# Attention with its q and k projections in plain fp32 instead of three fp32r products

## The chip, the cores and the metric

The kernel runs on one core of one Trainium2 chip. The metric is the device time of one execution in microseconds; the median of three runs of the kernel before is 1016.85 us. A profile is of one execution, with its own span and its own time.

## The reference

Only the first of three stages is touched. q, k and v are 4 x 8 x 576 x 64 (batch, heads, positions, head size), w_phi is 64 x 128:

```python
def phi(x):
    proj = np.einsum('bhsd,df->bhsf', x, w_phi)
    proj = proj - np.max(np.abs(proj), axis=-1, keepdims=True)
    return np.concatenate([np.exp(proj), np.exp(-proj)], axis=-1)
q_p, k_p = (phi(q), phi(k))
kv = np.einsum('bhsf,bhsd->bhfd', k_p, v)
z = np.sum(k_p, axis=2)
num = np.einsum('bhsf,bhfd->bhsd', q_p, kv)
den = np.einsum('bhsf,bhf->bhs', q_p, z)[..., None] + 1e-06
```

num / den, laid out as 2304 tokens of 512, goes through two feed-forward stages: relu(x w_in) squared times w_out (hidden size 2048), then sigmoid(x w_gate) * (x w_val) times w_out2 (hidden size 1536).

## The kernel before

Attention goes over 16 pairs of heads (4 batches, 4 pairs each; one pass of the loop over `n` is called an iteration here). Of a pair's 576 positions of k, 512 are taken as 4 x 128; the last 64 of all 8 heads of a batch are gathered in `kr` and done once a batch, in the first of its four iterations.

An iteration issues, in this order: `q_exp` of pair n (subtract the maximum, two exponentials); `proj_ks` and `proj_qs` of pair n + 1; `trans` of pair n + 2 (transposes of q and k on TensorE); `kv` of pair n (L373 and L380); `num` of pair n - 1 (L403 and L410, then the division on VectorE and GpSimd); `kv_tr` (L390); the loads of pair n + 3; in some iterations a weight conversion for the next stage (`convert1`) or a split of the attention output (`xsplit`), both mostly on VectorE. That is the order of the program; the framework then orders the instructions of each engine by a simulated timeline, so the code for the engines is fixed before the run.

A transposed tile stands in PSUM and is taken out by `split_evac`: ScalarE copies it rounded to fp32r (L289), VectorE subtracts that from the tile in PSUM and writes the rest, also fp32r (L290). So `qT`, `kT` and `krT` have two parts, and so have the weights `wq` and `wk`. A projection multiplies in three `passes`: high by high, high by low, low by high.

* `proj_k` (L347, three to six instructions each): one tile of 128 positions for two heads is the stationary operand (all 128 rows, 128 columns), and the weights move, 256 columns, set in blocks so that each half of the rows meets its own head's columns. Two such products of three passes make one `proj_k`: 6 instructions. There are 32 of them and 4 more for the remainder.
* `proj_q` (L326): for each of the two halves `e` of the positions the weights are stationary (64 rows, 128 columns) and 288 columns move. The two halves lie in partitions 0 to 63 and 64 to 127. 6 instructions for a head, 32 heads.

Everything else of attention is already plain fp32: L373, L380, L403, L410, the transposes L298, L305, L313 and L390, and the warm-up L258. All attention products use one pool of 8 PSUM banks (`bank`), so a product may have to wait until a bank is free. `proj_q` is taken out of PSUM by ScalarE (L329), `proj_k` by VectorE (L352, L353).

The feed-forward stages (L530, L551, L603, L707) follow, in fp32r with three passes, and are not touched.

Of the kernel before, what the change touches and what calls it, by code (L numbers as in the profile page):

```python
# [9 lines left out]
F32 = mybir.dt.float32  # L10
F32R = mybir.dt.float32r
U32 = mybir.dt.uint32
AF = mybir.ActivationFunctionType
ALU = mybir.AluOpType
# [5 lines left out]
def attention_moe_moe2(ctx, tc, q, k, v, w_phi, w_in, w_out, w_gate, w_val, w_out2, out):  # L20
    nc = tc.nc
    B, H, S, D = q.shape
    F = w_phi.shape[1]
    NT, DM = out.shape
    P = 128
# [20 lines left out]
    passes = ((0, 0), (0, 1), (1, 0))  # L46
    TINY = (2.0 ** -15 * 1.125) ** 2

    def f(ap):
        return ap.bitcast(F32)  # L50
# [8 lines left out]
    def bank(n):  # L59
        return ps.tile([P, 512], F32, tag="a", name="a")[:, :n]  # L60
# [30 lines left out]
    def split(hi, lo, src, hi_eng=nc.vector):  # L91
        if hi_eng is nc.scalar:
            nc.scalar.activation(hi, src, AF.Copy)  # L93
        else:
            hi_eng.tensor_copy(hi, src)
        last_g[0] = nc.vector.tensor_tensor(lo, src, f(hi), ALU.subtract)  # L96
# [120 lines left out]
    with ExitStack() as actx:  # L217
        cst = actx.enter_context(tc.tile_pool(name="cst", bufs=1))
# [3 lines left out]
        tp = tctx.enter_context(tc.tile_pool(name="tp", bufs=2, side="right"))  # L222
# [12 lines left out]
        for i in range(4):  # L235
            sl = slice(32 * i, 32 * i + 32)
            nc.vector.tensor_copy(ident[sl, sl], ramp[sl, 2])
        wst = cst.tile([P, F], F32, name="wst")
        for e in range(2):
            nc.scalar.dma_start(out=wst[e * D:(e + 1) * D, :], in_=w_phi)  # L240
        wq = cst.tile([P, 2, F], F32R, name="wq")
        split(wq[:, 0], wq[:, 1], wst)
        ones = cst.tile([P, 32], F32, name="ones")
        nc.vector.memset(ones, 1.0)
        zr = cst.tile([P, F], F32, name="zr")
        nc.vector.memset(zr, 0.0)
        wk = cst.tile([P, 2, 2, F], F32R, name="wk")
        for x in range(2):
            for e in range(2):
                nc.vector.tensor_copy(wk[:, x, e, :], zr)  # L250
        for x in range(2):
            for e in range(2):
                sl = slice(e * D, (e + 1) * D)
                nc.vector.tensor_copy(wk[sl, x, e, :], f(wq[sl, x, :]))

        warm = bank(P)
        for _ in range(NWARM):
# [26 lines left out]

        tT = {}

        def split_evac(pst, nm, key, bufs):
            t = tp.tile([P, 2, pst.shape[1]], F32R, tag=nm, name=nm, bufs=bufs)
            nc.scalar.activation(t[:, 0], pst, AF.Copy)  # L289
            nc.vector.tensor_tensor(t[:, 1], pst, f(t[:, 0]), ALU.subtract)  # L290
            tT[key] = t

        def trans_k(b, j):
            pt = bank(512)
            a = nat["k", b, j]
            for c in range(4):
                e, r = divmod(c, 2)
                nc.tensor.transpose(pt[:, c * P:(c + 1) * P], a[:, e, 2 * r:2 * r + 2, :], ident)  # L298
            split_evac(pt, "kT", ("k", b, j), 2)

        def trans_q(b, h):
            pt = bank(SH)
            a = nat["q", b, h // 2]
            for r in range(3):
                nc.tensor.transpose(pt[:, r * P96:(r + 1) * P96], a[:, h % 2, 2 * r:2 * r + 2, :], ident[:P96, :P96])  # L305
            split_evac(pt, "qT", ("q", b, h), 4)

        def trans_rem(b):
            a = nat["kr", b]
            pt = bank(NJ * SR)  # L310
            for j in range(NJ):
                o = (j % 2 * 2 + j // 2) * SR
                nc.tensor.transpose(pt[:, o:o + SR], a[:, 2 * j:2 * j + 2, :], ident[:SR, :SR])  # L313
            split_evac(pt, "krT", ("kr", b), 1)

        qx = {}
        mx = {}
# [2 lines left out]
        def proj_q(b, h):  # L320
            t = tT["q", b, h]
            pps = [bank(SH) for e in range(2)]
            for n, (x, y) in enumerate(passes):
                for e in range(2):
                    sl = slice(e * D, (e + 1) * D)
                    nc.tensor.matmul(pps[e], lhsT=wq[sl, x, :], rhs=t[sl, y, :], start=n == 0, stop=n == 2)  # L326
            for e in range(2):
                a = qpp.tile([P, 2, SH], F32, tag="qe", name="qe", bufs=12)
                nc.scalar.activation(a[:, 1, :], pps[e], AF.Copy)  # L329
                m = qpp.tile([P, SH], F32, tag="m", name="m", bufs=4)  # L330
                nc.gpsimd.partition_all_reduce(m, a[:, 1, :], channels=P, reduce_op=bass_isa.ReduceOp.absmax)  # L331
                qx[b, h, e] = a
                mx[b, h, e] = m
# [9 lines left out]
        def proj_k(t, o, key, tag, bufs):  # L343
            pp = bank(512)
            for r in range(2):
                for n, (x, y) in enumerate(passes):
                    nc.tensor.matmul(pp[:, r * 256:(r + 1) * 256], lhsT=t[:, x, o + r * P:o + (r + 1) * P],  # L347
                                     rhs=wk[:, y].rearrange("p a f -> p (a f)"), start=n == 0, stop=n == 2)
            a = pp.rearrange("p (c f) -> p c f", c=4)
            t = php.tile([P, 4, 2, F], F32, tag=tag, name=tag, bufs=bufs)  # L350
            m = sm.tile([P, 4, 1], F32, tag="km", name="km", bufs=3)
            nc.vector.tensor_reduce(m, a, AX.X, ALU.max, apply_absolute_value=True)  # L352
            nc.vector.tensor_tensor(t[:, :, 1, :], a, m.to_broadcast([P, 4, F]), ALU.subtract)  # L353
            nc.scalar.activation(t[:, :, 0, :], t[:, :, 1, :], AF.Exp)
            nc.scalar.activation(t[:, :, 1, :], t[:, :, 1, :], AF.Exp, scale=-1.0)
            ph[key] = t
# [76 lines left out]
        def trans(n):  # L433
            b, j = divmod(n, NJ)
            for e in range(2):
                trans_q(b, 2 * j + e)
            trans_k(b, j)
            if j == 0:
                trans_rem(b)

        def proj_qs(n):
            b, j = divmod(n, NJ)
            for e in range(2):
                proj_q(b, 2 * j + e)

        def proj_ks(n):
            b, j = divmod(n, NJ)
            for e in range(2):
                proj_k(tT["k", b, j], e * 256, (b, 2 * j + e), "ph", 4)
            if j == 0:  # L450
                proj_k(tT["kr", b], 0, ("r", b), "phr", 2)
# [16 lines left out]
        for n in range(B * NJ):  # L468
            b, j = divmod(n, NJ)
# [384 lines left out]
```

## Time and profile before

| | |
|---|---|
| median of 3 runs | 1016.85 us (1013.15 to 1017.01) |
| profiled execution, its own time | 1013.1 us |
| its span in the trace | 1011.3 us |
| TensorE (PE) busy | 991.6 us, 98% |
| VectorE (DVE) busy | 747.3 us, 74% |
| ScalarE (ACT) busy | 601.7 us, 59% |
| GpSimd (POOL) busy | 109.7 us, 11% |
| attention, until the first L530 | 198.5 us of the span |

The 1.8 us between the span and the time of the same execution lie outside the trace. A plain fp32 product appears in the trace as two PE MATMUL records (and two weight loads), an fp32r product and a transpose as one. Records of PE overlap, since matmuls are pipelined: the pace of PE is read from start to start, not from the duration of one.

### The profile page before, as it was taken

How to read it: one execution, taken by the hardware profiler on the slowest of the kernel's cores; microseconds unless marked ns; L12 is line 12 of the kernel's file. 1: busy time of each engine (PE TensorE's matmuls, PEld its weight loads, DVE VectorE, ACT ScalarE, POOL GpSimd, SP SyncE). 2: the span in 40 equal slices, each digit the busy share in tenths (PEclk: the TensorE clock that was granted, in tenths of full speed). 3: DMA queues.
4: the chain of work that ended last, by engine and by line, in shares of the span. 5: the costliest groups of instructions: out<-in, count | busy, mean ns of one | idle time of the engine just before them, and what ended most of it. 6: DMA issues, size and time to landing. Idle time of an engine off the chain costs nothing.

```text
span 1011.3 us, 17524 instructions
## 1 busy us (share of the span) xinstructions
PE 991.6 (98%) x6488; PEld 870.3 (86%) x6488; DVE 747.3 (74%) x1296; ACT 601.7 (59%) x1081; POOL 109.7 (11%) x196
## 2 busy tenths in 40 slices
PE   7999999999999999999999999999999999999996
PEld 6666666599999999889998899998899988999985
DVE  6799998869885987986969769856565656566532
ACT  6888878556555786446864466654465644555431
POOL 4556655400000000000000000000000000000000
PEclk9999999999999999999999999999999999999999
DMA  9444521349984576565775556632444422544302
GB/s 236 127 134 141 160 76 57 113 156 351 304 293 141 183 254 191 167 200 186 260 226 171 177 167 205 189 118 74 118 142 133 124 77 64 166 125 135 96 11 62
DMA packets 116406, 159.56 MB, mean 158 GB/s; under 512 B 12768, under 2 KB 74848, under 8 KB 116320
## 3 DMA queue, kind: packets, MB, share of 16 engines
q1 hardware_dynamic: 115680, 157.58, 49.8%
q8 instruction: 51, 0.84, 0.3%
q10 hardware_dynamic: 640, 0.85, 0.2%
q14 instruction: 35, 0.29, 0.1%
HBM read 125.37 MB, written 33.03 MB: 157 GB/s over the span
## 4 chain that ended last, share of the span: by engine, by line
PE 94%; DVE 3%; ACT 2%; POOL 0%; issue 0%; ACTq 0%
PE d L603 38%; PE d L551 20%; PE d L707 15%; PE d L530 7%; PE a L373 3%; PE a L410 3%; PE a L347 2%; PE a L380 2%; PE a L403 2%; PE a L326 1%; PE a L305 1%; PE a L390 1%; PE a L298 1%; ACT qe L329 0%; PE a L258 0%; ACT c L609 0%
## 5 line engine op out<-in xcount | busy, mean ns | idle before, releaser
L603 PE MATMUL d<-xs,hl 128*128 128x384 f32 x2184 | 385.4, 337 | 3.6 <-ACT c L609 3.6
L603 PEld LDWEIGHTS d<-xs,hl 128*128 128x128 f32 x2184 | 379.4, 188 | 6.6 <-ACT c L609 4.9
L138 DVE TENSOR_TENSOR hl<-wf,hl 128x512 fp32r<-128x512 f32 x282 | 192.4, 687 | 75.5 <-ACT hl L137 74.5
L137 ACT ACTIVATE hl<-wf 128x512 fp32r<-128x512 f32 x282 | 175.0, 626 | 88.5 <-PE d L603 48.3
L551 PE MATMUL d<-ghi,hl 128*128 128x256 f32 (+1 forms) x768 | 190.7, 338 | 0.0
L551 PEld LDWEIGHTS d<-ghi,hl 128*128 128x128 f32 x768 | 131.8, 188 | 16.3
L551 PE MATMUL d<-glo,hl 128*128 128x512 f32 (+1 forms) x384 | 128.5, 338 | 0.0
L707 PE MATMUL d<-hl,ghi 128*128 128x512 f32 x432 | 126.7, 395 | 0.0
L93 ACT ACTIVATE ghi<-G 128x768 fp32r<-128x768 f32 x48 | 40.7, 847 | 99.3 <-PE d L707 56.0
L707 PEld LDWEIGHTS d<-hl,ghi 128*128 128x128 f32 x432 | 80.9, 188 | 18.2
L96 DVE TENSOR_TENSOR glo<-G,ghi 128x768 fp32r<-128x768 f32 x48 | 46.0, 958 | 57.4 <-ACT ghi L93 56.9
L609 ACT ACTIVATE c<-d 128x768 f32<-128x768 f32 x78 | 61.3, 809 | 44.8 <-PE d L603 44.6
L331 POOL PARTITION_ALL_REDUCE m<-qe x64 | 83.5, 1375 | 35.5 <-ACT qe L329 33.3
L632 DVE TENSOR_TENSOR c<-c,d 128x768 f32<-128x768 f32 x54 | 51.2, 953 | 41.1 <-ACT c L609 26.8
L551 PEld LDWEIGHTS d<-glo,hl 128*128 128x128 f32 x384 | 72.3, 188 | 8.6
L707 PE MATMUL d<-hl,glo 128*128 128x512 f32 x216 | 76.3, 395 | 0.0
L530 PE MATMUL d<-xs,hl 128*128 128x384 f32 x384 | 69.1, 337 | 0.0
L530 PEld LDWEIGHTS d<-xs,hl 128*128 128x128 f32 x384 | 66.7, 188 | 1.1 <-issue 0.4
L115 ACT ACTIVATE st<-st 128x512 f32<-128x512 f32 x68 | 45.5, 678 | 32.4 <-DVE w L112 29.8
L707 PEld LDWEIGHTS d<-hl,glo 128*128 128x128 f32 x216 | 40.6, 188 | 9.8
L112 DVE SCALAR_TENSOR_TENSOR w<-st,w 128x512 uint32<-128x512 uint32 x68 | 46.6, 698 | 0.2
L113 DVE SCALAR_TENSOR_TENSOR w<-st,w 128x512 uint32<-128x512 uint32 x68 | 46.4, 693 | 0.5
(109 smaller groups left out, 1134.4 us busy)
## 6 DMA issues: line engine op xcount, KB each, us to landing
wf<-wd SPq DMA_DIRECT2D x84, 256.0 KB, 3.0
wf<-smd SPq DMA_DIRECT2D x72, 256.0 KB, 3.1
st<-in_moe_w_out_dram SPq DMA_DIRECT2D x28, 512.0 KB, 5.2
wf<-gvd SPq DMA_DIRECT2D x54, 256.0 KB, 3.2
wf<-wid SPq DMA_DIRECT2D x46, 256.0 KB, 4.3
st<-in_moe_w_in_dram SPq DMA_DIRECT2D x16, 512.0 KB, 5.9
wf<-ismd SPq DMA_DIRECT2D x32, 256.0 KB, 3.2
wd<-w SPq DMA_DIRECT2D x28, 256.0 KB, 3.4
```

Of the source, the lines that this page charges most:

```text
L96: last_g[0] = nc.vector.tensor_tensor(lo, src, f(hi), ALU.subtract)
L112: nc.vector.scalar_tensor_tensor(b, hi, 0xC0000000, b, ALU.bitwise_and, ALU.bitwise_or)
L113: nc.vector.scalar_tensor_tensor(b, lo, 29, b, ALU.logical_shift_right, ALU.bitwise_or)
L137: nc.scalar.activation(d[:, 0], a, AF.Copy)
L138: nc.vector.tensor_tensor(d[:, 1], a, f(d[:, 0]), ALU.subtract)
L331: nc.gpsimd.partition_all_reduce(m, a[:, 1, :], channels=P, reduce_op=bass_isa.ReduceOp.absmax)
L530: nc.tensor.matmul(pp[:, i, :n], lhsT=w[:, x, j, :], rhs=xs[j][:, y, o:o + n], start=k == 0, stop=k == 3 * NJ - 1)
L551: nc.tensor.matmul(acc[j][i], lhsT=w[:, x, j, :], rhs=a[y][:, o:o + n], start=c == 0 and k == 0 and (i == 0 or j % 2 == 0), stop=c == C1 - ...
L603: nc.tensor.matmul(acc[k, q][:, m], lhsT=w[:, i, 2 * m + kt, :], rhs=v[:, j, kt, :], start=start and n == 0, stop=n == 5, skip_group_check ...
L609: nc.scalar.activation(side[name, q], acc["X", q], AF.Copy)
L632: nc.vector.tensor_tensor(a, a, acc[k, q], ALU.add)
L707: nc.tensor.matmul(acc[u], lhsT=g[x][:, u * P:(u + 1) * P], rhs=w[:, y].rearrange("p j f -> p (j f)"), start=c == 0 and n == 0, stop=c == ...
```

## The change

The weights stay one fp32 tile each (`wst`, and `wk` with zeros around the two blocks), the transposed tiles are copied once by ScalarE into fp32 (`evac`), and each projection is one fp32 product instead of three fp32r ones.

```diff
-        wq = cst.tile([P, 2, F], F32R, name="wq")
-        split(wq[:, 0], wq[:, 1], wst)
+        wk = cst.tile([P, 2, F], F32, name="wk")
+        nc.vector.memset(wk, 0.0)
+        for e in range(2):
+            sl = slice(e * D, (e + 1) * D)
+            nc.vector.tensor_copy(wk[sl, e, :], wst[sl, :])
...
-        zr = cst.tile([P, F], F32, name="zr")
-        nc.vector.memset(zr, 0.0)
-        wk = cst.tile([P, 2, 2, F], F32R, name="wk")
-        for x in range(2):
-            for e in range(2):
-                nc.vector.tensor_copy(wk[:, x, e, :], zr)
-        for x in range(2):
-            for e in range(2):
-                sl = slice(e * D, (e + 1) * D)
-                nc.vector.tensor_copy(wk[sl, x, e, :], f(wq[sl, x, :]))
...
-        def split_evac(pst, nm, key, bufs):
-            t = tp.tile([P, 2, pst.shape[1]], F32R, tag=nm, name=nm, bufs=bufs)
-            nc.scalar.activation(t[:, 0], pst, AF.Copy)
-            nc.vector.tensor_tensor(t[:, 1], pst, f(t[:, 0]), ALU.subtract)
+        def evac(pst, nm, key, bufs):
+            t = tp.tile([P, pst.shape[1]], F32, tag=nm, name=nm, bufs=bufs)
+            nc.scalar.activation(t, pst, AF.Copy)
             tT[key] = t
...
-            for n, (x, y) in enumerate(passes):
-                for e in range(2):
-                    sl = slice(e * D, (e + 1) * D)
-                    nc.tensor.matmul(pps[e], lhsT=wq[sl, x, :], rhs=t[sl, y, :], start=n == 0, stop=n == 2)
+            for e in range(2):
+                sl = slice(e * D, (e + 1) * D)
+                nc.tensor.matmul(pps[e], lhsT=wst[sl, :], rhs=t[sl, :], start=True, stop=True)
...
-                for n, (x, y) in enumerate(passes):
-                    nc.tensor.matmul(pp[:, r * 256:(r + 1) * 256], lhsT=t[:, x, o + r * P:o + (r + 1) * P],
-                                     rhs=wk[:, y].rearrange("p a f -> p (a f)"), start=n == 0, stop=n == 2)
+                nc.tensor.matmul(pp[:, r * 256:(r + 1) * 256], lhsT=t[:, o + r * P:o + (r + 1) * P],
+                                 rhs=wk.rearrange("p a f -> p (a f)"), start=True, stop=True)
```

`trans_q`, `trans_k` and `trans_rem` call `evac` in place of `split_evac`, with the same names and numbers of buffers; the tiles are half as large.

## Rows read from the trace of the kernel before

**Rows 1.** The page: the chain that ended last, share of the span by engine.
```profile
PE 94%; DVE 3%; ACT 2%; POOL 0%; issue 0%; ACTq 0%
```

**Rows 2.** Windows: length, busy PE, PEld, DVE, ACT, POOL (instructions), PE clock, DMA share, GB/s.
```profile
12.00:24.00 12.00, 9.58 (x110) 7.02 (x108) 11.01 (x22) 11.19 (x29) 8.22 (x7) 1.00 1.14 262
...
60.00:72.00 12.00, 11.90 (x137) 7.69 (x134) 11.23 (x26) 10.02 (x25) 7.07 (x14) 1.00 0.51 156
```

**Rows 3.** The chain in order of time, at full clock: start, us, what.
```profile
95.06 2.11 PE a L347 x18
...
114.94 1.11 PE a L403 x16
116.05 2.09 PE a L410 x16
...
118.61 1.41 PE a L347 x12
120.02 0.64 PE a L326 x6
120.67 0.41 ACT qe L329
```

**Rows 4.** The same chain where it runs over DVE, first and last piece.
```profile
130.62 0.69 DVE km L352
...
156.05 0.59 DVE ph L353
```

**Rows 5.** Waits: PE's L305 in 30 to 178 us (us, times); PE after 170 us.
```profile
  ACT qe L329: 3.2, 11
...
PE d L603 <- ACT c L609: 3.6, 4, 0.9
```

**Rows 6.** Timeline of PE, 59.6 to 75 us: start, us, instruction.
```profile
62.10 1.07 PE L326 MATMUL a<-qT,wq 64*128 64x288 f32 x12
63.27 0.92 PE L305 MATMUL a<-ident,q 96*128 96x96 f32 x6
64.02 0.60 PE L298 MATMUL a<-ident,k 128*128 128x128 f32 x4
64.56 1.95 PE L373 MATMUL a<-ph,vx 128*64 128x256 f32 x16
...
71.88 1.67 PE L347 MATMUL a<-wk,kT 128*128 128x256 f32 x12
73.48 1.07 PE L326 MATMUL a<-qT,wq 64*128 64x288 f32 x12
74.65 0.60 PE L305 MATMUL a<-ident,q 96*128 96x96 f32 x4
```

**Rows 7.** Timeline of the start, all engines; of 8.6 to 16 us, PE alone.
```profile
3.69 3.78 PE L258 MATMUL a<-ident 128*128 128x128 f32 x16 [3.69 <-DVE ident L237]
...
7.26 0.98 PE L305 MATMUL a<-ident,q 96*128 96x96 f32 x6
...
8.73 0.40 PE L326 MATMUL a<-qT,wq 64*128 64x288 f32 x1
8.78 0.28 PE L313 MATMUL a<-ident,kr 64*128 64x64 f32 x2
...
9.35 0.69 DVE L290 TENSOR_TENSOR kT<-a,kT 128x512 fp32r<-128x512 f32 x1
...
10.47 1.46 PE L347 MATMUL a<-wk,kT 128*128 128x256 f32 x10
```

**Rows 8.** Groups by line, 30 to 178 us: busy us, mean ns.
```profile
L290 DVE TENSOR_TENSOR qT<-a,qT 128x288 fp32r<-128x288 f32 x26 | 11.0, 447 | 1.2 <-ACT qT L289 1.2
L290 DVE TENSOR_TENSOR kT<-a,kT 128x512 fp32r<-128x512 f32 x13 | 8.8, 677 | 0.0
```

**Rows 9.** Windows of 4 us around the first full iteration; columns as in Rows 2.
```profile
20.00:24.00 4.00, 2.65 (x48) 1.29 (x44) 3.01 (x6) 4.00 (x11) 2.37 (x2) 1.00 1.09 288
24.00:28.00 4.00, 3.95 (x24) 3.45 (x25) 2.64 (x5) 3.68 (x11) 0.00 (x0) 0.62 0.99 217
```

More of the change, by code (lines that the diff above doesn't have):

```diff
@@ L298, in trans_k @@
                 nc.tensor.transpose(pt[:, c * P:(c + 1) * P], a[:, e, 2 * r:2 * r + 2, :], ident)
-            split_evac(pt, "kT", ("k", b, j), 2)
+            evac(pt, "kT", ("k", b, j), 2)
         def trans_q(b, h):
@@ L305, in trans_q @@
                 nc.tensor.transpose(pt[:, r * P96:(r + 1) * P96], a[:, h % 2, 2 * r:2 * r + 2, :], ident[:P96, :P96])
-            split_evac(pt, "qT", ("q", b, h), 4)
+            evac(pt, "qT", ("q", b, h), 4)
         def trans_rem(b):
@@ L313, in trans_rem @@
                 nc.tensor.transpose(pt[:, o:o + SR], a[:, 2 * j:2 * j + 2, :], ident[:SR, :SR])
-            split_evac(pt, "krT", ("kr", b), 1)
+            evac(pt, "krT", ("kr", b), 1)
         qx = {}
```

## Prediction

> **What bounds the kernel now.** I read the chain of waits first, since the page's busy shares are averages over three stages. It is TensorE for 94% of the span [rows 1]: whatever this change takes from or adds to TensorE's own stream inside attention goes into the end, unless it falls into one of TensorE's gaps. So the next view is the windows of attention. From 24 us on TensorE is busy for all but about 0.1 us of a 12 us window, while VectorE has 11.2 and ScalarE 10.0 of the same 12 us [rows 2]. The reader should see two things there. VectorE is nearly full too, so it matters whether it paces TensorE. And 12 to 24 us is different: TensorE has 9.6 of 12, ScalarE 11.2 [rows 2], and the chain there runs over ScalarE.
>
> Does VectorE pace TensorE? Between 130.6 and 156 us the chain does run over VectorE [rows 4]. But a chain followed backwards takes the last releaser of one short wait and then stays on that engine; the waits of TensorE itself show how long it stood. In 30 to 178 us the transposes L305 waited 0.8 us in all for VectorE's L353, and in eleven places for ScalarE's L329, 3.2 us counted at the weight loads [rows 5]. That last one is the only gap of the steady state that repeats: about 0.2 us an iteration by the row's own sum, for a PSUM bank that the copy of the first head's projection must free. Behind 170 us TensorE waits for 3.6 us in four places that attention doesn't touch [rows 5]. So the answer is no: VectorE is close behind, and TensorE's own work sets the iteration.
>
> **What the change does, part by part.**
>
> *VectorE's L290 goes.* 447 ns for each of two q tiles and 677 ns for a k tile [rows 8]: 1.57 us an iteration, some 26 us in all with the remainders. What it hides behind is TensorE, and the previous paragraph says that TensorE stands for VectorE almost nowhere. Worth at the end: 0. The bound on the good side is all of TensorE's small gaps of the steady state, 14 iterations of 0.2 us, 2.8 us. I put 0.3 us of it into the sum, since banks that VectorE empties (L352, L430) come free sooner and some of the waits for a bank may go. ScalarE's L289 stays, one for one, with the same elements. After the change ScalarE, at 10.0 of 12 us, is the engine next to TensorE.
>
> *The projection of k on TensorE.* Before: three fp32r passes, 6 records for one `proj_k`. The chain gives 2.11 us for 18 records and 1.41 for 12 [rows 3], 0.117 us each with nothing left over for a start. After: 2 plain fp32 products, two records each, so 4 records of 256 columns. The price of such a record is read from products that are already plain fp32. L403 makes its 16 records four at a time (four column strips), 4 steps, in 1.11 us, and L410 two at a time, 8 steps, in 2.09 [rows 3]. Four steps more cost 0.98 us: 0.245 us for a step of 288 columns, and a fixed 0.13 us for a group. That is 0.85 ns a column, so 0.218 us for 256 columns. A second row agrees: four transposes of 128 columns, each full width as these records will be, take from 64.02 to 64.56 us with the change to the next kind of product in it [rows 6], at most 0.135 each, or 0.11 if the fixed 0.13 comes off, which is 0.22 for 256. With the rounding of these rows I take 0.217.
>
> An iteration has two `proj_k`: 12 x 0.117 = 1.41 us become 8 x 0.217 = 1.74, so +0.32. The remainder has one, +0.16. In the stretch where TensorE sets the pace stand the projections of pairs 2 to 15, 14 iterations and 3 remainders: 14 x 0.32 + 3 x 0.16 = **+5.0 us**. With 0.213 and 0.220 for a record the sum is 4.4 and 5.4.
>
> The Trainium skill (FP8 and Floating Point Precision, TensorE Precision Notes) says that true fp32 makes four passes through the array. By it, as an estimate, four passes against three would add a third to the bare streaming of both projections. The trace agrees in kind: a plain record costs 0.218 us against 0.117 for an fp32r one of the same width, and there are two of them for every three [rows 3]. The measured sum of k alone is smaller than a third, 0.32 of 1.41.
>
> *The projection of q on TensorE.* Before: two heads, 12 records that run in pairs, because the halves `e` use different rows of the array. After: 8 records, and if they pair too, 4 steps of 288 columns: 0.13 + 4 x 0.245 = 1.11 us until the transposes can start. Before, the chain gives 0.64 us for the first head, then 0.41 for ScalarE's copy that frees the bank, then L305 [rows 3], 1.10 in all with the gap between them; the timeline says 1.17 from the first start of L326 to that of L305, in two iterations [rows 6]. What is late next: after the change the first head is done at 0.13 + 2 x 0.245 = 0.62, its copy 0.41 later, so at 1.03, and the transposes then wait for TensorE's own second head at 1.11 rather than for the copy. So one product more in columns, and the same time: **0**, where the wait for the bank was. The three iterations in 14 that had no such wait have no cover, and pay up to 0.2 us each. For all 14, I keep -0.8 (0.06 less than 1.17 each) to +1.5 us (0.11 more each).
>
> Do they pair? The trace before has no plain fp32 product on half the rows beside one on the other half. It has the two nearest: fp32r on the two halves of the rows (12 records in 1.07 us [rows 6], where 288 columns at 0.42 ns, half of 0.85, would need 1.4 one by one), and plain fp32 on halves and quarters of the columns, where the arithmetic above holds only if they run together. And at 8.73 us an L326 record starts in the middle of the transposes L313, which use the other half of the rows [rows 7]. I take it that they pair.
>
> *The start.* `wk` and `wst` are set up with fewer instructions, before anything waits for them. The first k projection waited for L290 (9.35 to 10.04 us) before its main part at 10.47 [rows 7]; that hop goes, up to 0.7 us. Its 18 records and the next 12 then cost +0.8 us on TensorE. Behind it, until 24 us, ScalarE sets the pace [rows 2] and its work is unchanged. I take 0, between -0.7 and +0.8.
>
> *Sum.* 5.0 - 0.3 + 0 + 0 = +4.7 us. Against the profiled execution's own 1013.1 that is 1017.8. That execution stands at the low end of the three runs; against their median, 1016.85, the same step gives **1021.5 us**, 0.46% more.
>
> **Rivals.**
>
> *In strict order.* The program now names both records of half 0 before those of half 1. If TensorE starts records in program order, half 1 begins only with the second record of half 0, and two heads take 5 steps in place of 4: +0.245 us an iteration, +3.4, 1024.9 us. Against it: L403's four strips are named one after another, with two records each, and still take four steps and not the eight or more that strict order would make [rows 3]. The Trainium skill (TensorE: Matmul & The Clock Gate, Measured speedup vs the span model) says that matmuls start and end in program order, without reordering, which is this rival's rule. L403's step count speaks against it, if the program's order is that of the source. Chance 0.07.
>
> *No pairing at all.* 8 steps in place of 4, about +1 us an iteration, 14 of them: 1036 us. Chance 0.04.
>
> *A full-width record costs twice.* The warm-up L258, plain fp32 of 128 columns and full width, takes 3.57 us for 16 records until L305 starts [rows 7], 0.223 each, twice the price that I use. Then an iteration would pay 8 x 0.446 - 1.41 = +2.2 us: 1016.85 + 14 x 2.2 + 3 x 1.1 = 1051 us. But TensorE had done nothing before these records, and in the window 24 to 28 us, where the granted clock was 0.62 on the mean after a stretch with 2.65 of 4 us busy [rows 9], other lines are slow too; I read L258 as the lower of the clock's two levels (1.2 and 2.4 GHz). Chance 0.03.
>
> *Faster: full-width fp32 streams at fp32r's pace.* L403 and L410 use strips of the columns. If their 0.85 ns a column came from the strips, a full-width record might cost 0.109 us for 256 columns, and k would fall from 1.41 to 0.87 an iteration: 14 x 0.54 + 3 x 0.27 = 8.4 us less, 1008.5 us. It decides below 0.16 us for a record. The transposes, full width at 0.11 for 128 columns [rows 6], speak against it. Chance 0.03.
>
> *The slow clock goes.* If TensorE is held up less at 20 to 24 us, the clock need not fall after it; 24 to 28 us at 0.62 [rows 9] cost 1.5 us. 1020 us, or 1018 with all of the small gaps. ScalarE is full there (4.00 of 4) and its work is unchanged. Chance 0.05.
>
> **How the numbers follow.** The forecast has 0.78. A measurement of this kernel can tell about 0.5%, 5.1 us, from no change. The forecast's own range, from its bounds (4.4 to 5.4 for k, 0 to -2.8 for VectorE's gaps, -0.8 to 1.5 for q, -0.7 to 0.8 at the start, and the runs' own 4 us), is 1016 to 1026; its centre lies 0.4 us under the limit, so of its 0.78 I give 0.46 to no change and 0.32 to slower. With the rivals: slower 0.32 + 0.07 + 0.04 + 0.03 = 0.46 (strict order is 0.8%), same 0.46 + 0.05 = 0.51, faster 0.03. The range 1016 to 1026 holds strict order and the slow clock too; it leaves out the three far rivals (0.10) and the ends of the forecast.
>
> **What would show it.** L347's group: 8 records an iteration, about 1.74 us in the chain where it was 1.41. L326: 8 records in pairs a few ns apart, and about 1.1 us until L305 starts; a first record that starts alone would be strict order. VectorE about 9.6 of 12 us in a window. TensorE still full from 24 us on, and the first L530 4 to 5 us later than at 198.5. The forecast is wrong if TensorE shows gaps of more than 0.3 us an iteration, if a full-width record is not near 0.217 us, or if the feed-forward stages change their length by more than 1 us.

## The result and the profile after

The changed kernel takes 1025.02 us (median of 4 runs, 1024.44 to 1025.14) beside 1016.75 us before (also 4 runs, the three above among them): a ratio of 1.0085, with a 95% interval of 1.0067 to 1.0103. A second measurement of the same two kernels, with the experiments, gave 1021.63 beside 1013.56 us, 1.0073 (1.0055 to 1.0090). The ratios stand as they were computed together with their intervals; they differ a little from the quotients of the two medians (e4's medians below would give 1.0011). So the change costs about 8 us, where 4.7 were forecast. The time lies in the stated range; the likeliest case, no change within 0.5%, is missed on the slow side.

Three stretches of the profile after answer to what was shown of before. First the loop, as the chain of waits in order of time (start, us, what; lines L337, L317, L297, L400 are the old L347, L326, L305, L410). It answers to [rows 3].

```profile
118.01 1.11 PE a L393 x16
119.12 2.09 PE a L400 x16
121.21 0.37 PE a L380 x2
121.58 0.43 PE a L337 x2
122.01 0.11 PE a L380
122.12 1.30 PE a L337 x6
123.42 1.17 PE a L317 x8
124.59 0.65 PE a L297 x6
...
145.04 2.59 PE a L337 x12
```

The eight records of k take 0.43 + 1.30 = 1.73 us where twelve took 1.41, and with the remainder 2.59 where 2.11. ScalarE's copy no longer stands between L317 and L297. The timeline has q's records as one group; it answers to [rows 6].

```profile
64.69 1.24 PE L317 MATMUL a<-qT,wst 64*128 64x288 f32 x8
65.86 0.71 PE L297 MATMUL a<-ident,q 96*128 96x96 f32 x6
```

From the first L317 to the first L297 are 1.17 us, as before. Next the start, in the timeline of all engines; it answers to [rows 7].

```profile
4.26 0.22 DVE L245 COPY wk<-wst 64x128 f32<-64x128 f32 x1 [1.62 <-DMA wst<-in_w_phi_dram]
...
4.40 0.72 DVE L237 COPY ident<-ramp 32x32 f32<-32x32 f32 x4
...
5.17 3.78 PE L251 MATMUL a<-ident 128*128 128x128 f32 x16 [5.17 <-DVE ident L237]
```

The reader should see the order on VectorE. The copies that make the identity matrix (L237) stand behind a copy into `wk`, which waits 1.62 us for the DMA of `w_phi`. Before, the warm-up began at 3.69 us [rows 7].

Last the end of attention, again the timeline.

```profile
200.23 2.16 PE L400 MATMUL a<-qe,kvs 128*64 128x288 f32 x16
...
203.66 0.78 DVE L420 TENSOR_TENSOR u<-a,rr 128x288 f32<-128x288 f32 x2
...
204.49 14.34 PE L520 MATMUL d<-xs,hl 128*128 128x384 f32 x72 [2.10 <-DVE u L420]
```

The first product of the feed-forward stage waits 2.10 us for VectorE's last division, and then takes 14.34 us for 72 records. The kernel before, profiled again, shows neither; these are pieces of its chain of waits: the first and the last full start of `kv`, and the first feed-forward product.

```profile
29.37 2.46 PE a L373 x20
...
178.40 2.53 PE a L373 x20
198.03 12.68 PE d L530 x72
```

The same three pieces of the changed kernel:

```profile
31.31 2.46 PE a L363 x20
...
183.25 2.46 PE a L363 x20
...
204.49 14.34 PE d L520 x72
```

So the first `kv` starts 1.94 us later, the 13 iterations between the two take 151.94 us in place of 149.03 (2.91 more), from the last `kv` to the feed-forward stage are 21.24 us in place of 19.63 (1.61 more), and the first product there takes 1.66 us more. That is 8.1 us. One thing behind it is not put down to the change: the records of L603 (L593) came to 385.4 us of busy time in most profiles and to 389.6 in this one and e7's, while a second profile of the changed kernel (e9) has 386.1. No profile of the kernel before has 389.6 itself, but its medians moved between measurements by about as much. So each experiment is read from its ratio to the runs of before made beside it, and from its trace up to the first feed-forward product.

### The profile page after: what moved, and what is told of

Its sections match the earlier page's. It is cut to its first block, busy times and chain, and to the rows that moved or that the text cites. A ratio compares the mean times of both kernels' runs of the same rounds, so it can differ in the third digit from the quotient of the medians.

```text
span 1023.1 us, 17181 instructions
## 1 busy us (share of the span) xinstructions
PE 1000.8 (98%) x6352; PEld 870.5 (85%) x6352; DVE 733.7 (72%) x1236; ACT 596.4 (58%) x1081; POOL 108.1 (11%) x196
## 4 chain that ended last, share of the span: by engine, by line
PE 96%; ACT 2%; DVE 1%; DMA 0%; ACTq 0%; issue 0%; POOL 0%; POOLq 0%
PE d L593 38%; PE d L541 20%; PE d L697 15%; PE d L520 7%; PE a L363 4%; PE a L400 3%; PE a L337 3%; PE a L370 2%; PE a L393 2%; PE a L317 2%; PE a L297 1%; PE a L380 1%; PE a L290 1%; PE a L251 0%; DMA wst<-in_w_phi_dram 0%; ACT c L599 0%
## 5 line engine op out<-in xcount | busy, mean ns | idle before, releaser
L593 PE MATMUL d<-xs,hl 128*128 128x384 f32 x2184 | 389.6, 339 | 3.6 <-ACT c L599 3.6
L593 PEld LDWEIGHTS d<-xs,hl 128*128 128x128 f32 x2184 | 383.6, 188 | 6.6 <-ACT c L599 4.9
L322 POOL PARTITION_ALL_REDUCE m<-qe x64 | 81.4, 1343 | 56.6 <-ACT qe L320 52.5
L520 PE MATMUL d<-xs,hl 128*128 128x384 f32 x384 | 70.7, 342 | 2.1 <-DVE u L420 2.1
L520 PEld LDWEIGHTS d<-xs,hl 128*128 128x128 f32 x384 | 68.3, 192 | 3.2 <-DVE u L420 2.6
L113 DVE SCALAR_TENSOR_TENSOR w<-st,w 128x512 uint32<-128x512 uint32 x68 | 48.1, 718 | 0.5
L116 DVE SCALAR_TENSOR_TENSOR w<-st,w 128x512 f32<-128x512 f32 x68 | 46.5, 690 | 0.8
```

The source lines that it names most:

```text
L113: nc.vector.scalar_tensor_tensor(b, lo, 29, b, ALU.logical_shift_right, ALU.bitwise_or)
L116: nc.vector.scalar_tensor_tensor(a, h, TINY, a, ALU.is_ge, ALU.mult)
L520: nc.tensor.matmul(pp[:, i, :n], lhsT=w[:, x, j, :], rhs=xs[j][:, y, o:o + n], start=k == 0, stop=k == 3 * NJ - 1)
L593: nc.tensor.matmul(acc[k, q][:, m], lhsT=w[:, i, 2 * m + kt, :], rhs=v[:, j, kt, :], start=start and n == 0, stop=n == 5, skip_group_check ...
```

## The experiments

**Another PSUM tile for the first feed-forward product (e1).** In the built program of the changed kernel the last product L400 lies in bank 0, and the first tile of the feed-forward stage in banks 0 and 1. The traces don't show banks; whether they matter is what this run and e10 test. One tile of that pool is taken first and written by one column, so that the product moves to banks 6 and 7.

```diff
+    skipped = dbl()
+    nc.vector.memset(skipped[:, 0, :1], 0.0)
     fetch_for(1)
     for s in range(C1 + 2):
```

> The changed kernel, with one PSUM tile taken and given a one-column write by VectorE before the first feed-forward product, so that this product's tile comes from banks 6 and 7 instead of 0 and 1; TensorE's order is the same. Theory A (the last attention product lies in bank 0, so the first feed-forward product waits for VectorE's L420, and the clock falls behind that wait): the wait of 2.1 us in front of the first L520 goes, its 72 records take about 12.7 us instead of 14.3, and the time falls by 3 to 4 us, from 1025.0 to about 1021.5. Theory B (the first feed-forward product needs something else of the end of attention, a weight or a split tile): the wait stays or is taken over by another, and the time is within 1 us of 1025.

Measured: 1016.82 beside 1012.64 us, a ratio of 1.0039 (1.0027 to 1.0052). The chain of waits has the last `kv` and the product:

```profile
183.14 2.46 PE a L363 x20
202.28 12.68 PE d L520 x72
```

The wait is gone, from the last `kv` to the product are 19.14 us in place of 21.24, and the 72 records take 12.68 us. Against the changed kernel's 1.0073 to 1.0085 that is 3.4 to 4.6 thousandths, as theory A said.

**The identity ahead of the weights (e2).** The copies into `wk` are queued on VectorE behind those of the identity.

```diff
-            nc.vector.tensor_copy(ident[sl, sl], ramp[sl, 2])
+            made = nc.vector.tensor_copy(ident[sl, sl], ramp[sl, 2])
...
-        for e in range(2):
-            sl = slice(e * D, (e + 1) * D)
-            nc.vector.tensor_copy(wk[sl, e, :], wst[sl, :])
+        with tc.issue_after(made.ins):
+            for e in range(2):
+                sl = slice(e * D, (e + 1) * D)
+                nc.vector.tensor_copy(wk[sl, e, :], wst[sl, :])
```

> The changed kernel, with the two copies that fill wk queued on VectorE behind the four copies that make ident. Theory A (ident stands behind a copy that waits for the DMA of w_phi, so the warm-up and all behind it start 1.4 us late): L251 starts at about 3.7 us instead of 5.17, the first full iteration starts 1 to 1.4 us earlier, and the time falls by 1 to 1.4 us. Theory B (until 24 us ScalarE and the loads set the pace, the late ident is hidden): L251 starts at 3.7 us, but the first L363 stays at 31.3 us and the time too. The PSUM wait at the end of attention stays as it is by both.

Measured: 1018.54 beside 1012.64 us, 1.0048 (1.0034 to 1.0062), 2.5 to 3.7 thousandths under the changed kernel. That is more than theory A has, but it can't be put down to the start: in the profiled execution the first feed-forward product took only 12.75 us, and the first `kv` is hardly earlier. The chain has the warm-up at 3.46 us, and the windows show why the gain was lost (length, busy PE, PEld, DVE, ACT, POOL, then the granted clock):

```profile
3.46 3.79 PE a L252 x16
31.16 2.46 PE a L364 x20
```

```profile
16.00:20.00 4.00, 3.85 (x10) 2.66 (x12) 2.37 (x5) 3.16 (x8) 0.00 (x0) 0.57 1.09 349
```

In this execution TensorE ran at a mean granted clock of 0.57 in these 4 us, with 3.85 of them busy: most of the time at the lower of its two levels; in the 4 us before, 2.43 us were busy. The third run settles it.

**Both edits (e3).**

> The changed kernel with both edits, the other PSUM tile for the first feed-forward product and wk's copies behind ident. If both theories A hold, 4.5 to 5 us less than 1025.0, about 1020.3, which is 0.35% more than before and leaves what the projections cost on TensorE, 14 x 0.32 + 3 x 0.16 = 5.0 us less the small gaps that went. If the costs are not these, nearer to 1025.

Measured: 1015.01 beside 1012.64 us, 1.0024 (1.0015 to 1.0033). Its chain:

```profile
29.05 2.46 PE a L364 x20
...
180.99 2.46 PE a L364 x20
200.12 12.68 PE d L521 x72
```

The warm-up starts at 3.45 us, 1.91 us earlier than with e1's edit alone (5.36), and the first `kv` 2.15 us earlier (31.20 in e1). In neither profile does the clock fall between 4 and 32 us. So the late identity was not hidden behind ScalarE. What is left against before is the loop, 151.94 us in place of 149.03. Theory A of both edits holds: of some 8 us, about 5 were the start and the end.

**k alone in plain fp32 (e4), q alone (e5).** From the kernel before; in e4 with both edits. `evac` is the changed kernel's.

```diff
 e4
-            split_evac(pt, "kT", ("k", b, j), 2)
+            evac(pt, "kT", ("k", b, j), 2)
... (krT, wk and proj_k as in the change)
 e5
-            split_evac(pt, "qT", ("q", b, h), 4)
+            evac(pt, "qT", ("q", b, h), 4)
... (proj_q as in the change)
```

> The kernel before with k alone in plain fp32 (kT and krT copied once), q still in three fp32r passes; wk's copies behind ident and the first feed-forward tile in other PSUM banks, as in the run with both edits. Theory A (the loss of the loop is k's: 8 records at 0.216 us for 12 at 0.118): a full iteration has 0.32 us more in L347 and the transposes L390 that stand among them; VectorE loses 0.68 us of an iteration, less than half of what the change took, so some of its gaps stay: 1015 to 1017 us on a chip where before takes 1012.6, at least as much as both together (1015.0). Theory B (k and q cost about equally): half of the 2.4 us, about 1013.8.

> The kernel before with q alone in plain fp32 (qT copied once), k still in three fp32r passes. Theory A (q costs nothing, as its second head ends when the transposes could start anyway, and VectorE's freed 0.9 us an iteration close gaps): L326 to L305 stays at 1.17 us, the transposes lose their breaks, and the time is 0 to 1.8 us below before, 1011 to 1012.6. Theory B (q costs a step of its pairs): up to 0.11 us an iteration more, 1013 to 1014.

Measured: e4 1015.66 beside 1014.57 us, 1.0001 (0.9990 to 1.0012); e5 1014.97 beside 1014.57, 1.0006 (0.9992 to 1.0019). e4's first theory misses in the time: it had at least e3's loss. e5's interval, about 0.8 us below to 1.9 above, doesn't tell its two theories apart. Two pieces of e4's chain:

```profile
83.54 1.73 PE a L347 x8
85.27 0.99 PE a L327 x12
...
97.83 0.64 PE a L327 x6
98.47 0.41 ACT qe L330
```

k costs its 0.32 us here as well. But in about half of the iterations no wait for a bank stands behind q, and then the split q needs 0.99 us and not 1.17: q's plain fp32 costs nothing only where that wait covers it. By the trace e4's loop is 150.88 us (28.99 to 179.87), between before and both, and its first feed-forward product starts at 199.43, 1.4 us behind before; its runs can't tell this from nothing. In e5 L330 to L310 (the old L326 and L305) stays at 1.17 us (84.86 to 86.03) and the loop is 149.15 us (29.34 to 178.49) beside 149.03. The breaks within the transposes are gone, as expected, yet waits in front of them came in their place. Most are in the view of the waits of the transposes, which have line L310 there (us, times; 4.8 us of it are counted at the weight loads):

```profile
  DVE u L434: 6.0, 11
```

Freed of 0.9 us an iteration, VectorE still held a bank too long in eleven places. TensorE's products themselves waited for it 1.2 us, in three places.

**VectorE's work given back (e6).** Both edits, and a subtraction of the old size behind each copy; nobody reads its output.

```diff
             nc.scalar.activation(t, pst, AF.Copy)
+            u = tp.tile([P, pst.shape[1]], F32, tag=nm + "d", name=nm + "d", bufs=1)
+            nc.vector.tensor_tensor(u, pst, t, ALU.subtract)
             tT[key] = t
```

(and one more tile skipped in front of the feed-forward stage)

> The run with both edits, and behind each copy out of PSUM a subtraction on VectorE of the same size as the old L290, into a tile that nobody reads; the tile's PSUM bank is held until it is done, as before. The output is the same. Theory A (VectorE's freed time is worth about 1.8 us over the loop, the gaps that went): the gaps in front of and within the transposes come back, and the time is 1.5 to 2.5 us above 1015.0. Theory B (VectorE is hidden behind TensorE all through, and the gaps went for another reason, q's shorter stream): within 0.5 us of 1015.0.

Measured: 1022.12 beside 1014.57 us, 1.0062 (1.0046 to 1.0078), so 3.8 thousandths above e3. TensorE, which waited for nothing between 30 and 180 us in the changed kernel, has waits again (engine, line, what for: us, times, longest), and the chain runs over VectorE:

```profile
PE a L300 <- DVE u L423: 2.1, 5, 0.5
PE a L293 <- PE a L300: 0.3, 1, 0.3
```

```profile
57.60 0.44 DVE qTd L285
...
58.65 0.60 DVE kTd L285
```

By the trace the loop is 156.25 us (29.49 to 185.74), 4.3 us above e3's. So VectorE's freed time is worth something, theory A; it is worth more here than the 1.5 to 2.5 us expected. Why the same subtraction costs more beside plain fp32 projections than beside split ones was not pursued.

**k by halves of the rows (e7, e8).** The zero blocks of `wk` make half of k's products idle. Both edits, and two products of 64 rows for each 128 positions, into two banks, as q has it; `kv` reads the tiles in the new order, and the remainder keeps `wk`.

```diff
+            pps = [bank(512) for e in range(2)]
+            for c in range(4):
+                for e in range(2):
+                    sl = slice(e * D, (e + 1) * D)
+                    nc.tensor.matmul(pps[e][:, c * F:(c + 1) * F], lhsT=t[sl, c * P:(c + 1) * P],
+                                     rhs=wst[sl, :], start=True, stop=True)
```

> The run with both edits, with k's projection split by halves of the rows like q's: for each of the four tiles of 128 positions two products of 64 rows and 128 columns, one for each half, into two PSUM banks, so that wk's zero blocks are no longer multiplied (the remainder keeps wk). If halves of the rows run together for plain fp32 as q's do, 8 steps of 128 columns at 0.109 us take the place of 8 of 256 at 0.216: 0.86 us less an iteration, as much as 13 us over the loop, of which VectorE (about 9.6 of 12 us) and ScalarE (10) should let most through: 1003 to 1006 us. If they don't pair at 128 columns, because each needs a weight load of 128 columns in front, 1013 to 1016.

Measured: 1015.98 beside 1014.57 us, 1.0008 (0.9995 to 1.0021), a gain against e3's 1.0024, but a small one; by the trace the first feed-forward product starts at 196.56 us, 3.6 us before e3's. The time is the one expected if the halves didn't pair, but they do, as the chain of e8 below shows. Two iterations of e7's chain, in pieces:

```profile
35.54 0.42 PE a L355 x4
35.96 0.26 PE a L402
36.22 0.87 PE a L355 x12
37.09 0.97 PE a L318 x8
...
63.20 2.46 PE a L385 x20
...
70.58 0.41 PE a L355 x2
71.00 0.26 PE a L402
71.26 0.97 PE a L355 x13
72.23 1.08 PE a L318 x8
```

The sixteen records L355 together need 1.09 us where they stand in one piece, and a transpose L402 behind others of its kind about 0.10 (in e8 below). Here a full-width transpose L402 cuts the records of k, and the two together come to 1.55 us in the first iteration and 1.65 in the second. In the second the cut goes through a pair: two records take 0.41 us, as long as four in the first, and q behind them needs 1.08 us in place of 0.97. So an iteration loses about 0.35 us to the transpose between whole pairs, and 0.55 where it cuts a pair too. e8 queues the projections behind all transposes of `kv_tr`, and takes the feed-forward tile from banks 4 and 5.

```diff
-                proj_ks(n + 1)
-                proj_qs(n + 1)
+                with tc.issue_after(turned[0].ins) if n else ExitStack():
+                    proj_ks(n + 1)
+                    proj_qs(n + 1)
```

(`turned[0]` is the last transpose of `kv_tr`)

> The run with k's projection in halves of the rows, with the projections of pair n + 1 queued on TensorE behind all three transposes of kv_tr, and the first feed-forward tile in banks 4 and 5. In that run a transpose L402 stands among the pairs in ten iterations of 14 and costs about 0.2 us on either side; the one iteration of the loop's end without it has 0.55 us less. Theory A (each change between halves of the rows and the full array drains TensorE, and that ate the pairing's gain): 10.65 us for a plain iteration in place of 11.20, the first feed-forward product at about 189 us instead of 196.6, 7 us less over the kernel. Theory B (VectorE, at 10.6 of 12 us, is the next bound): iterations of 11 us or more with gaps in front of L355 or L298, at most 3 us less.

Measured: 1008.77 beside 1013.56 us, 0.9944 (0.9925 to 0.9962): faster than both kernels. Its chain:

```profile
64.32 2.46 PE a L385 x20
...
71.34 0.47 PE a L402 x3
71.82 1.09 PE a L355 x16
72.91 0.97 PE a L318 x8
...
74.97 2.46 PE a L385 x20
```

An iteration is 10.65 us where e7's is 11.20 (63.20 to 74.40) and the changed kernel's 11.48 (114.19 to 125.67). The first feed-forward product starts at 194.09 us, not at the expected 189. The iterations with a remainder still cost 11.95 to 12.64 us, and in this execution the first full `kv` starts 2.5 us later than e7's (30.62 and 28.15), with mean granted clocks of 0.83 and 0.74 from 24 to 32 us. The loop itself is 143.85 us beside e7's 148.86; the direction is theory A's.

**Each kernel once more (e0, e9), and the wait put into the kernel before (e10).** e0 is the kernel before and e9 the changed one, without an edit. e10 is the kernel before with two tiles skipped in front of the feed-forward stage, so that its first product falls into bank 4, where before's last L410 lies.

> The kernel before, unchanged, profiled once more. In the first trace of it the records of L603 are 173 ns apart, in the changed kernel's half of them 179: 4.2 us more over the feed-forward stages. Theory A (a state of TensorE's stream that changes from execution to execution, and the first trace caught the before kernel at its fastest, 1013.1 us): a profile at about 1016.8 us shows L603 records of 179 ns, and the first L530 still at 198.4 us. Theory B (the change makes L593 slower): every profile of the before kernel has 173 ns, and its 3.7 us lie elsewhere, in attention.

> The changed kernel, unchanged, profiled once more beside before. Theory A (feed-forward takes 743.0 or 747.2 us in one execution or another, whichever kernel it is, and the clock's fall behind the wait at the end of attention comes in some executions): the first L520 is at 204.5 us again, the rest 743.0 or 747.2 us or near; before's runs show both levels, and so do those of the changed kernel. Theory B (747.2 us belongs to the changed kernel): 747.2 us again, and no run of it under 1023 us.

> The kernel before, with two PSUM tiles taken and written by one column before the first feed-forward product, so that this product's tile comes from banks 4 and 5, and the last attention product lies in bank 4. Theory A (the wait at the end of attention is a matter of which bank the first tile falls into): a wait for VectorE's L430 in front of the first L530 appears, which starts 1.7 to 2.1 us later than at 198.0 to 198.4 us, and its 72 records take 12.7 us, or up to 14.3 where the clock falls: 1.7 to 3.7 us more than before. Theory B (the wait belongs to the changed kernel's longer attention): no wait, no change.

Measured: e0 1012.64 beside 1012.64 us, 1.0000 (0.9991 to 1.0008), with 385.4 us of L603; the higher figure didn't appear in it, so its two theories stay open. e9 1021.63 us, 1.0073 as told above, with the first L520 at 204.49 us, 14.33 us for its 72 records and 386.1 us of L593, neither of the two levels; one run of six is above 1023. So theory B of e9 is out, and A right only in that the number moves. e10 1016.93 beside 1013.56 us, 1.0030 (1.0017 to 1.0043). Its waits, and the product in its chain:

```profile
PE d L530 <- DVE u L430: 2.1, 1, 2.1
```

```profile
200.14 14.33 PE d L530 x72
```

The same wait of 2.1 us, then the same 14.33 us, with none of the change in the kernel: 2.1 + 1.65 = 3.8 us in this execution. Theory A of e10 holds.

## Why the prediction was right or wrong

**What bounds the kernel: right for the loop.** TensorE's own stream sets it. After the change TensorE waits for nothing between 30 and 180 us.

**k: right.** Forecast 1.41 to 1.74 us an iteration and +0.16 for the remainder; measured 1.73, and 2.59 in place of 2.11. Over the 13 iterations counted here, with three remainders, that is 13 x 0.32 + 3 x 0.16 = 4.6 us. The forecast's second row was misread (0.54 us less 0.13 gives 0.10 us for 128 columns, not 0.11); the first row's 0.218 us for a record was right, at 0.216.

**q: right in the sum.** The halves pair, and L317 to L297 is 1.17 us. e4 shows the cover that the forecast named: without the wait for the bank the split q needs 0.99 us. So q costs 0.1 us over the loop by itself (e5), but 1.06 us on top of k (e3's 151.94 beside e4's 150.88), which the forecast's range held and its 0 did not.

**L290: mis-sized.** The sum had -0.3 us for VectorE's share, with 2.8 as the bound. Over the 13 iterations the loop grew by 2.9 us where k alone is 4.6, so 1.7 us of small losses went. TensorE's idle time in these iterations fell from 1.10 us to 0; the other 0.6 us isn't located. With k alone (e4) the loop grew by 1.85 us, so 2.8 went there, and q took 1.1 of it back. In e6 TensorE is idle for 2.47 us again, with waits for VectorE, but the loop grew by more than had gone: that the gaps hang on VectorE is borne out, their size is not. VectorE was also freed by less than the forecast took. L290 for q and k was 19.7 us in these iterations, yet VectorE's busy time fell only from 133.91 to 125.85 us: the subtractions of the maximum (L337, now L328) took 676 ns each in place of 497, 8.3 us more in all. e3's and e9's profiles have the same; the cause stays open.

**The start: wrong.** "I take 0", with a bound of +0.8. The forecast said that `wk` and `wst` are set up "before anything waits for them". It counted instructions and didn't ask in which order VectorE has them: a copy that waits for a DMA now stood ahead of the identity, and the warm-up on TensorE began at 5.17 us in place of 3.69. The first `kv` came 1.94 us later, beyond the bound. e1 and e3, apart by this edit, have their first `kv` at 31.20 and 29.05 us.

**The end of attention: missing.** The forecast had no term behind the loop; it expected the first feed-forward product 4 to 5 us late, and that the stages behind wouldn't change by over 1 us. The product came 6.5 us later than in before's second profile, and its own 72 records took 1.66 us more. A wait of 2.1 us for a PSUM bank was new (e1 takes it away, e10 puts it into the kernel before), and behind it the clock fell. The 1.6 us between the last `kv` and the product are this wait less 0.5 us that the stretch gained (19.14 us in e1 beside 19.63). The windows of the changed kernel there:

```profile
200.00:204.00 4.00, 2.39 (x24) 1.06 (x16) 2.15 (x8) 0.53 (x1) 1.48 (x8) 1.00 0.01 4
204.00:208.00 4.00, 3.51 (x14) 3.51 (x15) 1.91 (x6) 0.00 (x0) 0.00 (x0) 0.70 0.00 0
208.00:212.00 4.00, 4.00 (x22) 4.00 (x21) 0.00 (x0) 0.00 (x0) 0.00 (x0) 0.87 0.00 0
```

TensorE had 2.39 of 4 us of work, and the lower of its two clock levels then held for part of the next 8 us. At half speed, the two means of 0.70 and 0.87 lose (0.30 + 0.13) x 4 = 1.7 us. e2 has the same wait, and its first product took 12.75 us, so the fall doesn't follow each time.

**The rivals.** Strict order, at 1024.9 us, came nearest to the time and is still wrong: eight records of q would then take five steps, over 1.3 us, and 1.17 were measured. No pairing and the doubled record are out by the same rows, and so is faster fp32 by k's 0.216 us a record (1.73 / 8). That the time met one rival's number shows why a rival needs a row of its own, and not only a time. The slow clock's condition came true and its gain didn't come: from 20 to 32 us the changed kernel's granted clock is 1.00. It is 1.00 there in the second profile of the kernel before, too, and the first `kv` then starts at 29.37 us in place of 29.89, so by these two profiles the fall had cost about 0.5 us and not 1.5.

**The sum.** Loop 2.9, start 1.9, end 1.6, clock 1.7: 8.1 us by the traces, 8.1 to 8.3 by the runs. Forecast were 5.0 - 0.3 for the first and 0 for the rest. That the time lies in the stated range is therefore luck in good part: the loop cost less than forecast, and the start and the end, which make up 5.2 of the 8.1 us, were taken as 0 or had no term.

## What to carry to other kernels

A change inside a scheduled kernel also moves what the scheduler derives from it: the order of setup work on an engine, and the bank into which the next stage's first tile falls. Here these two came to 5.2 us where the loop came to 2.9, and both could be mended by an edit of a few lines, so check the first and the last microseconds of a stage before judging the edit itself. Before replacing a cheap product by an exact one, see whether half of its columns or rows are multiplied by zeros; dropping those paid for the exact product and more, once the full-width work was kept out from among the halves.

## What was not expected of the hardware

* A full-width transpose among products on halves of the rows cost about 0.55 us an iteration (11.20 against 10.65 us), 0.2 of it by cutting a pair. The Trainium skill (TensorEngine Tiling (Array Packing), Key Properties) says that changing the tiling mode drains TensorE, and changing the tile within a mode does not. The chains of e7 and e8 agree: k's halves followed by q's halves run through (1.09 and 0.97 us in e8), with a transpose among them k's need 1.55 us or more, the transpose included.
* After a wait of about 2 us the 72 records of the first feed-forward product took 14.33 or 14.34 us in three profiles (the changed kernel's two and e10's) and 12.75 in a fourth (e2's), with the same wait.
* L603, untouched, had 385.4, 386.1, 386.5 or 389.6 us of busy time in profiles of different kernels (389.6 in the changed kernel's first and in e7's). What sets it stays open.
* VectorE's subtraction of the maximum, the same instruction on 128x288 elements, took 676 ns on the mean in the changed kernel and 497 in the kernel before, where VectorE had more to do. What sets it stays open.
